# Gated linear attention before a SoLU block: the first loads split by halves of heads over two queues, narrower products of ones, and part of w_in requested later

## The chip, the cores and the metric

One NeuronCore of a Trainium2 chip (trn2). The metric is the device time of one execution in microseconds (us); lower is better. A NeuronCore has five engines with a queue of instructions each: TensorE (PE, matrix products), VectorE (DVE), ScalarE (ACT), GpSimd (POOL) and SyncE (SP), which in this kernel mostly issues DMAs. 16 DMA engines move the data. The engines run independently and wait for each other by semaphores.

## What is computed

Inputs q, k, v and alpha have the shape 4 x 8 x 768 x 48 (batch, head, position, width). The first block is a recurrence over the positions, the second works on the 3072 tokens of 8 x 48 = 384 numbers that come out of it.

```python
for t in range(S):
    state = alpha[:, :, t, :, None] * state + np.einsum('bhd,bhe->bhde', k[:, :, t], v[:, :, t])
    y[:, :, t] = np.einsum('bhd,bhde->bhe', q[:, :, t], state)
...
h = x @ w_in                                  # 3072 x 384 times 384 x 1024
e = np.exp(h - h_max)
solu = h * (e / (np.sum(e, axis=-1, keepdims=True) + 1e-09))
ln = (solu - mu) / np.sqrt(var + 1e-06) * g_ln
return (ln @ w_out).astype(np.float32)        # 1024 x 384
```

The weights w_in, w_out and g_ln reach the kernel in double or single precision; here w_in and w_out are double, and the kernel makes single precision of them itself.

## The kernel before

The positions are cut into six groups of 128 (g = 0 to 5). Group 0 has a prologue of its own, written out by hand in one fixed order; later groups' attention is interleaved with the second block of the group before, by a table of steps. The order of each engine's instructions is the order in which the program writes them; nothing reorders them afterwards. Where a buffer or a semaphore is shared, the instruction waits.

The prologue of group 0, which the change touches, goes as follows.

- Loads. `load_first` (L146) requests alpha, then k, then q for the first 128 positions on SP's queue, each in two requests of two batches. A request of two batches is 16 x 128 pieces of 192 bytes, one for each head and position. `load_v` (L176) requests v in four. ACT's queue brings ident, mask, parity and g_rows (L671 to L675), four small constants. Then `fetch` (L578) requests the first pieces of w_in: `fetch(0, 3)` into slot 3 of `room`, `fetch(1, 4)` into slot 4, `fetch(2, 1, 2)` two pieces into slots 1 and 2. Each is three requests.
- `warm` (L452) multiplies a tile of ones by itself 14 times on PE. A single-precision product passes twice, so these are 28 passes. The result is not used.
- `turned` (L164) turns a loaded tile [position, batch x head x width] so that the width lies on the partitions: 12 blocks of 4 batches, each a product with ident. Blocks 0 to 7 are the first 32 numbers of heads 0 to 7. Blocks 8 to 11 are the other 16 numbers of pairs of heads; they are first gathered by an ACT copy, `ends_of` (L155). The results are three PSUM tiles of four blocks each: tp_a0 (heads 0 to 3), tp_a1 (heads 4 to 7), tp_a2 (the ends). For k and q they are tp_k and tp_q.
- Alpha's three tiles are copied to aT by ACT (L703), and DVE runs a scan over each (`scan_back`, L204), which gives the products of alpha from the end of the group. `alpha_over` (L196) checks on ACT that alpha is at most 1. After `inverses` (a reciprocal, L213), `scan_on` scans a second time (L204 too), for each tile.
- DVE multiplies the turned k by the first scan (kT, L712) and the turned q by the second (qv and qe, L721). From qe, ACT makes two masked versions (`apart`, L245).
- `scores` (L278) multiplies kT and qv on PE, in two halves of heads; `masked` (L289) sets the upper part to zero on DVE, with a quarter of it on ACT and POOL (`masked_apart`, L297 and L298). `read_values` (L333) multiplies by v, and ACT copies the result to x (L363).
- `bits(0)` makes single precision of the first piece of w_in with five DVE instructions (L616 to L630); `keys_back` (L303) turns the keys back.
- Then the second block starts: `up_mm` (L394) multiplies w_in and x for eight slices f of 128 columns, the first two of which need the first piece of w_in only. `bits(1)` makes the second piece, and so on. `down` (L507) is the second product, with w_out.

The order in the prologue is then: loads, `warm(14)`, alpha turned, copied and scanned, k turned, `alpha_over`, `inverses`, a scan, kT, a scan, `warm(4)`, q turned, qv, qe, `apart`, a scan, qv, the scores, the masks, `bits(0)`, `read_values`, `keys_back`, `up_mm`.

Of the kernel before, what the change touches and what calls it, by code (L numbers as in the profile page):

```python
# [16 lines left out]
P = 128  # L17
# [15 lines left out]
def fast_path(ctx, tc, q, k, v, alpha, moe_w_in, moe_w_out, moe_g_ln, out):  # L33
# [12 lines left out]
    nc = tc.nc  # L46
    B, H, S, D = q.shape
# [4 lines left out]
    NP = H // 2  # L52
    NB = H + NP
# [8 lines left out]
    def pool(name, bufs, **kw):  # L62
        return ctx.enter_context(tc.tile_pool(name=name, bufs=bufs, **kw))
# [8 lines left out]
    ps_o = pool("ps_o", 2, space=PS)  # L72
# [4 lines left out]
    ident = const.tile([P, P], FP, name="ident")  # L77
    mask = const.tile([P, P], FP, name="mask")
    ones = const.tile([P, P], FP, name="ones")
    small_ones = const.tile([P, 32], FP, name="small_ones")  # L80
    parity = const.tile([P, 2], FP, name="parity")
# [9 lines left out]
    slots = [room[:, 1536 * i : 1536 * i + 1536] for i in range(6)]  # L91
# [7 lines left out]
    an = const.tile([P, H, TQ, D], FP, name="an")  # L99
# [39 lines left out]
    def by_token(x):  # L139

        return x.rearrange("p h u d -> p (h u d)").rearrange("p (b h d) -> p b h d", b=B, h=H)

    def load_first(src, dst, g):
        t = slice(g * P, (g + 1) * P)
        for b in range(0, B, 2):
            nc.sync.dma_start(  # L146
                out=by_token(dst)[:, b : b + 2].rearrange("p b h d -> p (b h) d"),
                in_=src[b : b + 2, :, t].rearrange("b h p d -> p (b h) d"),
            )

    def ends_of(src, tag=None):

        ends = ring.tile([P, T4], FP, name=tag) if isinstance(tag, str) else lots[tag][:, 0:T4]
        ends = ends.rearrange("p (b d) -> p b d", b=B)
        nc.scalar.copy(out=ends.rearrange("p b (h d) -> p b h d", h=H), in_=by_token(src)[:, :, :, E0:D])  # L155
        return ends

    def turned(src, ends, out, blocks=range(NB)):

        x = by_token(src)  # L160
        for j in blocks:
            for b in range(B):
                cols = x[:, b, j, 0:E0] if j < H else ends[:, b, E0 * (j - H) : E0 * (j - H) + E0]
                nc.tensor.matmul(  # L164
                    out[j // NP][32 * b : 32 * b + 32, j % NP], lhsT=cols, rhs=ident, start=True, stop=True,
                    tile_position=(0, 32 * b), skip_group_check=True,
                )
# [38 lines left out]
    def scan_back(g, i):  # L206

        part = slice(NP * i, NP * i + NP)
        scan(h4[:, part], aT[:, part], unit, True)
# [5 lines left out]
    def scan_on(g, i):  # L215
        part = slice(NP * i, NP * i + NP)
        scan(aT[:, part], aT[:, part], seed[:, part], False)
# [25 lines left out]
    def apart():  # L243
        for i in range(2):
            nc.scalar.mul(  # L245
                out=qv[:, H : 2 * H, 0:P].rearrange("p (j i) t -> p j i t", i=2)[:, :, i], in_=qe[:, :, 0:P],
                mul=parity[:, i : i + 1],
            )
# [16 lines left out]
    def quarter(b):  # L265
        return slice(32 * b, 32 * b + 32)

    def banks(name, shape, n=B):
        return [ps_a.tile([P] + shape, FP, tag=f"a{b}", name=f"{name}{b}") for b in range(n)]

    def scores(g, half, a=None):
        a = a or banks("a", [NP, P])
        for last in range(2):
            for i in (0, 2, 1, 3):
                h = half * NP + i
                kb, qb = (H + h // 2, H + h) if last else (h, h)
                for b in range(B):
                    nc.tensor.matmul(  # L278
                        a[b][:, i], lhsT=kT[quarter(b), kb], rhs=qv[quarter(b), qb, 0:P], start=not last and not i, stop=bool(last),
                        tile_position=(32 * b, 0), skip_group_check=True,  # L280
                    )
        masks[half] = a
# [163 lines left out]
                nc.scalar.copy(out=d["p"][:, i], in_=d["q"][i])  # L446
            d["unit"] = small_ones

    def warm(n, ps=ps_o, tag="o"):
        t = ps.tile([P, 512], FP, tag=tag, name="warm")  # L450
        for i in range(n):
            nc.tensor.matmul(t[:, 0:P], lhsT=ones, rhs=ones, start=True, stop=True)  # L452

    def token_sums(g):

# [111 lines left out]
    def fetch(i, slot, n=1):  # L567

        kind, f = pieces[i]
        w = n * F // (2 if kind else KC)  # L570
        raw = room[:, 1536 * slot : 1536 * (slot + n)].bitcast(U32).rearrange("p (c f w) -> p c f w", f=w, w=2)
        if kind:
            parts = [(slice(0, P), c, moe_w_out[(f + c) * P : (f + c + 1) * P, :]) for c in range(2)]
        else:
            parts = [(slice(0, P), c, moe_w_in[c * P : (c + 1) * P, f * P : f * P + w]) for c in range(KC)]
        for rows, c, src in parts:
            if float64:
                nc.sync.dma_start(out=raw[rows, c].rearrange("p f w -> p (f w)"), in_=src.bitcast(U32))  # L578
            else:
                dst = w_out[rows, f + c, 0:DM] if kind else w_in[rows, c, f * P : f * P + w]  # L580
                nc.sync.dma_start(out=dst, in_=src)
        for m in range(n):
            raws[i + m] = raw[:, :, w // n * m : w // n * (m + 1)]
# [81 lines left out]
    def inline(x, name):  # L665
        return nc.inline_tensor(np.ascontiguousarray(x, np.float32), name=name).ap()

    load_first(alpha, an, 0)
    nc.vector.memset(mone, -1.0)
    nc.scalar.activation(out=far[:, 0, 1:2], in_=mone, func=AF.Exp)  # L670
    nc.scalar.dma_start(out=ident, in_=inline(np.eye(P), "ident_c"))  # L671
    nc.scalar.dma_start(out=mask, in_=inline(np.triu(np.ones((P, P))), "mask_c"))
    odd = np.arange(P) // E1 % 2
    nc.scalar.dma_start(out=parity, in_=inline(np.stack([1 - odd, odd], 1), "parity_c"))
# [10 lines left out]
    nc.gpsimd.memset(kg, 0.0)  # L685
    load_v(0)
    fetch(0, 3)
    fetch(1, 4)
    fetch(2, 1, 2)
    nc.vector.memset(ones, 1.0)  # L690
    nc.vector.memset(small_ones, 1.0 / 32)
    nc.vector.memset(mhalf, -0.5)
# [2 lines left out]
    def three(name, where):  # L695
        return [pool.tile([P, NP, P], FP, tag=tag, name=f"{name}{i}") for i, (pool, tag) in enumerate(where)]


    warm(14)
    t = three("tp_a", [(ps_a, "a0"), (ps_a, "a1"), (ps_a, "a2")])  # L700
    turned(an, ends_of(an, 1), t)
    for i in range(3):
        nc.scalar.copy(out=aT[:, NP * i : NP * i + NP, 1:SW], in_=t[i])  # L703
        scan_back(0, i)
    t = three("tp_k", [(ps_a, "a3"), (ps_h, "h"), (ps_h, "h")])
# [7 lines left out]
    scan_on(0, 0)  # L713
    t = three("tp_q", [(ps_a, "a0"), (ps_o, "o"), (ps_o, "o")])
    warm(4, ps_a, "a1")
    turned(qn, ends_of(qn, 3), t, (*range(NP), *range(H, NB), *range(NP, H)))
    for i in (0, 2, 1):
        if i == 1:
            scan_on(0, i)
        part = slice(NP * i, NP * i + NP)  # L720
        nc.vector.tensor_tensor(  # L721
            out=qe[:, :, 0:P] if i == 2 else qv[:, part, 0:P], in0=t[i], in1=aT[:, part, 1:SW], op=ALU.mult
        )
        if i == 2:
            apart()
    scores(0, 0)
    t = [x.tile([P, NP, P], FP, tag=n, name="a_" + n) for x, n in ((ps_h, "h"), (ps_o, "o")) for _ in range(2)]
    scores(0, 1, t)
# [193 lines left out]
    for g in range(1, G + 1):  # L922
# [10 lines left out]
        for s in range(FC):  # L933
# [18 lines left out]
            if todo:  # L952
                n, half = todo.pop(0)
# [24 lines left out]
    def compare(out, x, bound, op):  # L978
# [6 lines left out]
        out=chunks[:, :, 2], in0=sums[:, :, 2], scalar=0.25, in1=sums[:, :, 3], op0=ALU.mult, op1=ALU.is_le  # L985
# [6 lines left out]
    else:  # L992
# [9 lines left out]
        out=bad, in0=all_ok[0:1, 0:1], scalar1=float(P * ends[-1]), scalar2=None, op0=ALU.is_lt  # L1002
# [415 lines left out]
def kernel(tc, *args):  # L1418

    with ExitStack() as ctx:  # L1420
        taken = fast_path(ctx, tc, *args)
    with tc.If(taken > 0):
        general_path(tc, *args)
# [30 lines left out]
```

## Time and profile before

| | |
|---|---|
| median of 3 runs | 368.23 us (368.16 to 368.46) |
| the profiled execution's own time | 367.97 us |
| its span (first to last instruction of the program) | 366.2 us |
| granted clock of TensorE, mean | 1.00 |
| PE busy, share of the span | 357.8 us, 98% |
| start of the first up-projection (L394) | 28.39 us |

The tables that follow come from this one profiled execution. In rows of the timeline, the first number is the start in us from the beginning of the span, the second the length in us, then come engine, line of the code, operation, the tile written and the tiles read, the shape and how many instructions are merged in the row; a bracket says how long the engine had been idle before and what ended the wait. PEld is the loading of weights into PE, which overlaps PE's own work. A name such as SPq is the queue of an engine that issues DMAs.

### The profile page before, as it was taken

The page shows a single profiled execution, that of the slowest core. Times are in us where ns is not written, and L with a number is a line of the kernel's source. Part 1 is how long each engine was busy: PE and PEld are TensorE (multiplying, and loading weights), DVE is VectorE, ACT ScalarE, POOL GpSimd, SP SyncE. Part 2 cuts the span into 40 slices and gives each one's busy share as a digit, 9 for nine tenths or more (in the row PEclk, how much of TensorE's full clock was granted, in tenths as well). Part 3 has the DMA queues.
Part 4 walks back from the last instruction along what each step waited for, and adds up shares of the span by engine and source line. Part 5 has one row for each costly group of instructions (what it writes and reads, how often), then busy time and mean ns, then how long its engine had stood idle before and what let it go on. Part 6 is the DMA issues. An engine that isn't in the chain of part 4 may idle for free. (4 is left out here: it accounts for less than half of the span.)

```text
span 366.2 us, 10036 instructions
## 1 busy us (share of the span) xinstructions
PE 357.8 (98%) x4341; PEld 215.0 (59%) x4341; DVE 245.0 (67%) x375; ACT 146.4 (40%) x260; POOL 132.2 (36%) x129
## 2 busy tenths in 40 slices
PE   8899999999999999999999999999999999999994
PEld 8784355666755566566575456475556565555552
DVE  0999989979998797936675935766946314345420
ACT  3647878182645262252521252431241132222110
POOL 7020000004449963774133764232773121233300
PEclk9999999999999999999999999999999999999999
DMA  9995995326196409463035354004041000000011
GB/s 180 183 338 152 204 309 124 88 67 159 50 234 141 109 21 180 85 152 94 21 92 112 83 121 126 3 25 88 21 107 55 0 25 0 24 21 22 23 47 51
DMA packets 72871, 36.06 MB, mean 98 GB/s; under 512 B 48232, under 2 KB 70000, under 8 KB 72816
## 3 DMA queue, kind: packets, MB, share of 16 engines
q1 hardware_dynamic: 71792, 34.39, 39.8%
q10 hardware_dynamic: 1024, 0.92, 0.8%
q8 instruction: 36, 0.59, 0.7%
q14 instruction: 19, 0.16, 0.2%
HBM read 25.30 MB, written 4.72 MB: 82 GB/s over the span
## 5 line engine op out<-in xcount | busy, mean ns | idle before, releaser
L507 PE MATMUL o<-w_out,room 128*128 128x385 f32 x384 | 134.0, 492 | 0.0
L394 PE MATMUL h<-x,w_in 128*128 128x512 f32 x288 | 131.7, 597 | 0.5 <-DVE g_col L642 0.5
L507 PEld LDWEIGHTS o<-w_out,room 128*128 128x128 f32 x384 | 71.0, 189 | 54.7 <-issue 13.1
L394 PEld LDWEIGHTS h<-x,w_in 128*128 128x128 f32 x288 | 53.2, 189 | 58.6 <-issue 48.5
L409 DVE TENSOR_TENSOR room<-h,e 128x512 f32<-128x512 f32 x40 | 27.5, 689 | 72.9 <-ACT e L408 72.9
L408 ACT ACTIVATE e<-h 128x512 f32<-128x512 f32 x40 | 24.0, 599 | 100.2 <-PE h L394 100.2
L427 POOL TENSOR_TENSOR p<-p,e 128x512 f32<-128x512 f32 x30 | 43.7, 1458 | 20.0 <-ACT e L408 19.9
L412 ACT ACTIVATE u<-room 128x512 f32<-128x512 f32 x40 | 25.2, 630 | 38.3 <-DVE room L409 38.3
L546 POOL TENSOR_TENSOR r<-sums,mhalf 128x1 f32<-128x1 f32 x20 | 14.8, 741 | 69.7 <-DVE sums L537 69.4
L289 DVE TENSOR_TENSOR sT<-a,mask 128x512 f32<-128x512 f32 x43 | 26.7, 681 | 8.0 <-PE a L278 7.9
L204 DVE TENSOR_TENSOR_SCAN hT<-aT,unit 128x516 f32<-128x516 f32 x18 | 24.4, 1399 | 7.6 <-ACT aT L703 7.5
L204 DVE TENSOR_TENSOR_SCAN aT<-aT,seed 128x516 f32<-128x516 f32 x18 | 27.4, 1551 | 0.2
L225 POOL TENSOR_TENSOR kT<-kT,hT 128x1024 f32<-128x1024 f32 (+1 forms) x8 | 14.2, 1800 | 32.7 <-DVE kT L179 32.7
L427 DVE TENSOR_TENSOR p<-p,u 128x512 f32<-128x512 f32 x30 | 22.5, 749 | 5.1 <-ACT u L412 5.1
L278 PEld LDWEIGHTS a<-qv,kT 32*128 32x128 f32 x704 | 21.4, 186 | 7.0 <-issue 2.6
L278 PE MATMUL a<-qv,kT 32*128 32x128 f32 x704 | 23.9, 278 | 0.4 <-POOL qv L253 0.3
L212 POOL COPY fend<-hT 128x12 f32<-128x12 f32 x6 | 3.1, 509 | 55.9 <-DVE hT L204 55.9
L333 PE MATMUL y<-sT,vn 128*32 128x128 f32 x768 | 22.6, 273 | 0.2 <-DVE sT L289 0.2
L333 PEld LDWEIGHTS y<-sT,vn 128*32 128x32 f32 x768 | 20.7, 110 | 1.6 <-issue 1.0
L196 ACT ACTIVATE sq<-an,mone 128x1536 uint8<-128x1536 f32 x12 | 18.9, 1572 | 0.2
L548 ACT ACTIVATE o_sb<-o,r 128x384 f32<-128x384 f32 x16 | 9.3, 582 | 18.5 <-POOL r L546 18.5
L261 POOL TENSOR_TENSOR state<-state,lot 128x384 f32<-128x384 f32 x10 | 8.8, 903 | 13.1 <-DMA lot<-qv 13.1
(148 smaller groups left out, 374.3 us busy)
## 6 DMA issues: line engine op xcount, KB each, us to landing
vn<-in_v_dram SPq DMA_DIRECT2D x24, 192.0 KB, 4.7
an<-in_alpha_dram SPq DMA_DIRECT2D x20, 192.0 KB, 4.1
out_dram<-o_sb SPq DMA_DIRECT2D x20, 192.0 KB, 1.9
room<-in_moe_w_out_dram SPq DMA_DIRECT2D x8, 384.0 KB, 5.5
kn<-in_k_dram SPq DMA_DIRECT2D x16, 192.0 KB, 5.6
qn<-in_q_dram SPq DMA_DIRECT2D x16, 192.0 KB, 4.1
lot<-qe SPq DMA_DIRECT2D x40, 64.5 KB, 2.1
lot<-qv SPq DMA_DIRECT2D x20, 129.0 KB, 2.4
```

What stands on the lines that cost most here:

```text
L196: nc.scalar.activation(out=sq, in_=x, func=AF.Relu, scale=sign, bias=mone, accum_out=over[:, g, i : i + 1])
L204: nc.vector.tensor_tensor_scan(out=o, data0=a, data1=s, initial=1.0, op0=ALU.mult, op1=ALU.add)
L278: nc.tensor.matmul(a[b][:, i], lhsT=kT[quarter(b), kb], rhs=qv[quarter(b), qb, 0:P], start=not last and not i, stop=bool(last), tile_posit ...
L289: nc.vector.tensor_tensor(out=sT[:, b, half * NP : half * NP + NP], in0=a[b], in1=mask[:, None, :].to_broadcast([P, NP, P]), op=ALU.mult,)
L333: nc.tensor.matmul(y_bank(b)[quarter(r), a], lhsT=lhsT, rhs=rhs, start=(b, r) not in begun, stop=stop, tile_position=(row, 32 * r), skip_g ...
L394: nc.tensor.matmul(h, lhsT=w_in[:, a, f * P : (f + 1) * P], rhs=d["x"][:, a].rearrange("p b t -> p (b t)"), start=(a == 0), stop=(a == KC ...
L408: nc.scalar.activation(out=e, in_=h, func=AF.Exp)
L409: nc.vector.tensor_tensor(out=u, in0=h, in1=e, op=ALU.mult)
L412: nc.scalar.activation(out=u2, in_=u, func=AF.Square)
L427: eng.tensor_tensor(out=p, in0=d[0][i] if f == 1 else p, in1=d[f][i], op=ALU.add)
L507: nc.tensor.matmul(d["o"][:, 0 : DM + 1], lhsT=u_of(g, f)[:, b * P : b * P + P], rhs=w_out[:, f], start=(f == 0), stop=(f == FC - 1), skip ...
L546: nc.gpsimd.tensor_tensor(out=r, in0=s[:, 3:4], in1=mhalf, op=ALU.pow)
```

## The change

Four edits, all in the prologue of group 0.

- The request for ident is the first on ACT's queue. After it, alpha is requested in eight parts instead of two: first heads 0 to 3 of each batch, then heads 4 to 7; batches 0 and 1 on SP's queue, batches 2 and 3 on ACT's. The table load of ACT and the requests for mask, parity and g_rows come behind.
- `warm` has a width; the first 14 products are of 92 instead of 128 columns. The later `warm(4)` stays at 128.
- Blocks 0 to 3 of alpha are turned, copied and scanned before the gathering copy of the ends. The other eight blocks are turned after it.
- `fetch(1, 4)` and `fetch(2, 1, 2)` move behind `apart`. A copy of one column of parity into slot 4 stands before them, so that the first of these requests has to wait for ACT to reach it. The other loads keep their order.

```diff
-    def warm(n, ps=ps_o, tag="o"):
+    def warm(n, ps=ps_o, tag="o", w=P):
         t = ps.tile([P, 512], FP, tag=tag, name="warm")
         for i in range(n):
-            nc.tensor.matmul(t[:, 0:P], lhsT=ones, rhs=ones, start=True, stop=True)
+            nc.tensor.matmul(t[0:w, 0:w], lhsT=ones[:, 0:w], rhs=ones[:, 0:w], start=True, stop=True)
...
-    load_first(alpha, an, 0)
+    nc.scalar.dma_start(out=ident, in_=inline(np.eye(P), "ident_c"))
+    for h in (slice(0, NP), slice(NP, H)):
+        for b in range(B):
+            queue = nc.sync if b < 2 else nc.scalar
+            queue.dma_start(out=by_token(an)[:, b, h], in_=alpha[b, h, 0:P].rearrange("h p d -> p h d"))
     nc.vector.memset(mone, -1.0)
     nc.scalar.activation(out=far[:, 0, 1:2], in_=mone, func=AF.Exp)
-    nc.scalar.dma_start(out=ident, in_=inline(np.eye(P), "ident_c"))
     nc.scalar.dma_start(out=mask, in_=inline(np.triu(np.ones((P, P))), "mask_c"))
...
     fetch(0, 3)
-    fetch(1, 4)
-    fetch(2, 1, 2)
...
-    warm(14)
+    warm(14, w=92)
     t = three("tp_a", [(ps_a, "a0"), (ps_a, "a1"), (ps_a, "a2")])
-    turned(an, ends_of(an, 1), t)
     for i in range(3):
+        if i == 0:
+            turned(an, None, t, range(NP))
+        elif i == 1:
+            turned(an, ends_of(an, 1), t, range(NP, NB))
         nc.scalar.copy(out=aT[:, NP * i : NP * i + NP, 1:SW], in_=t[i])
         scan_back(0, i)
...
         if i == 2:
             apart()
+            nc.scalar.copy(out=slots[4][:, 0:1], in_=parity[:, 0:1])
+            fetch(1, 4)
+            fetch(2, 1, 2)
```

## Prediction

> **What bounds the kernel now.** I read the page first, then a table by stage (the windows view), then the timeline of the first 30 us, last the DMA packets of that stretch.
>
> ```profile
> PE 357.8 (98%) x4341; PEld 215.0 (59%) x4341; DVE 245.0 (67%) x375; ACT 146.4 (40%) x260; POOL 132.2 (36%) x129
> ```
>
> TensorE is busy 98% of the span. The windows view says where the rest lies (columns: window, length, then busy us and instructions of PE, PEld, DVE, ACT, POOL, then clock, DMA share and GB/s):
>
> ```profile
> 0.00:6.80 6.80, 5.45 (x32) 5.06 (x32) 0.29 (x5) 1.49 (x2) 6.21 (x12) 1.00 0.89 167
> 6.80:12.10 5.30, 4.38 (x153) 4.12 (x157) 3.46 (x3) 3.90 (x6) 0.49 (x1) 1.00 1.13 186
> 28.40:366.00 337.60, 332.53 (x3748) 192.26 (x3748) 225.69 (x345) 132.40 (x238) 122.69 (x113) 1.00 0.37 88
> ```
>
> From 28.4 us on, where the up-projection starts, PE works 332.5 of 337.6 us, so that part is bound by PE and is only shifted by what happens before it. Only the first 28.4 us are open, and every 0.1 us by which the first up-projection (L394) starts sooner is 0.1 us of the total. In the prologue the chain goes by these rows of the timeline (start, length):
>
> ```profile
> 6.83 1.83 PE L164 MATMUL tp_a<-ident,an 128*32 128x128 f32 x58 [0.30 <-DMA an<-in_alpha_dram]
> 8.64 3.48 DVE L204 TENSOR_TENSOR_SCAN hT<-aT,unit 128x516 f32<-128x516 f32 x3 [7.54 <-ACT aT L703]
> ...
> 14.99 0.96 PE L164 MATMUL tp_q<-ident,qn 128*32 128x128 f32 x26 [0.20 <-DMA qn<-in_q_dram]
> 15.41 1.22 DVE L204 TENSOR_TENSOR_SCAN aT<-aT,seed 128x516 f32<-128x516 f32 x1
> 16.74 0.69 DVE L721 TENSOR_TENSOR qv<-tp_q,aT 128x512 f32<-128x512 f32 x1
> 17.35 0.68 DVE L721 TENSOR_TENSOR qe<-tp_q,aT 128x512 f32<-128x512 f32 x1
> 17.73 2.45 PE L278 MATMUL a<-qv,kT 32*128 32x128 f32 x64
> 18.07 1.34 ACT L245 ACTIVATE qv<-qe,parity 128x512 f32<-128x512 f32 x2 [2.42 <-DVE qe L721]
> ...
> 23.91 0.76 DVE L616 TENSOR_SCALAR lot<-room 128x768 uint32<-128x768 uint32 x1
> 28.39 2.81 PE L394 MATMUL h<-x,w_in 128*128 128x512 f32 x6 [0.46 <-DVE g_col L642]
> ```
>
> VectorE sits idle 7.54 us until alpha is turned, then runs almost without a gap to 28.2: three scans to 12.12, one more, keys, a scan to 16.64, qv, qe, and so on. The last step before L394 is the making of w_in's first piece (L616 to L630, 23.91 to 28.24). So **two clocks run side by side**: the VectorE chain, which alpha starts, and the load queue, which brings q at 14.95 and the first piece of w_in at 23.52 (last of its three transfers, by the landings in the trace). Slack of the second against the first is small: q's third block was turned at 16.93 and used at 17.35; w_in was there 0.39 us before its use.
>
> ```profile
> GB/s 0 0 0 18 178 271 265 274 236 233 225 210 221 222 219 199 226 226 208 227 218 227 97 21 124 255 260 246 199 202 223 104 157 214 127 183 198 133 117 131
> ```
>
> This row is the DMA rate in half-microseconds from 0 to 20 us: the engines work from 1.85 us without rest except for a hole near 11.5. The loads are a stream at its own pace.
>
> [...] SP spends 1.67 to 1.76 us on each 2048-packet request between 4.7 and 8.2, but only 1.47 on one after the hole, so it can issue faster than it does. [...] between 2.75 and 3.0 us alpha's packets fall from 270 to 183 per quarter while 77 of ident's pass. [...] Here products of ones start at 1.08 and the clock rises at 4.71, 3.63 us later; it never falls.
>
> **The change, part by part.**
> Narrower products (L452). 28 passes of 128 columns come every 213 ns until 4.71, then every 112. With 92 columns I scale to 92/128: 153 and 80 ns. 23 passes are through by 4.71, the other five by 5.15. PE is free at about 5.2 instead of 6.19. The 36 columns fewer cost nothing: no result is used.
>
> Alpha by halves on two queues. Alpha is 4096 packets of 192 B either way: two requests on SP become four on SP and four on ACT. The first half with ident is 2048 + 128 packets; before, the first 2048 and ident had landed at 4.64. I take 4.7. So PE turns heads 0 to 3 from 5.2: 32 passes at 27.3 ns (the spacing in tp_a) and 0.27 to drain end at 6.35; the copy (L703, 0.59) ends at 7.0, and the first scan starts at 7.05 instead of 8.64. The other half lands with all of alpha; mask, parity and g_rows (136 packets of 512 B, 128 tiny) now queue behind it, which by their 21 to 26 ns each over 16 engines is worth 0.25: 6.55 instead of 6.79. ACT copies the ends after aT0 (7.0 to 7.6), tp_a1 ends at 7.7 and is copied to 8.35, tp_a2 ends at 8.8 and is copied to 9.45. Scans at 7.05, 8.4, 9.55, ending at 10.75: **1.37 us sooner than 12.12**. Reciprocal, scan, three key products and scan keep their 4.5 us and end at 15.3 (before 16.64).
>
> ACT's queue. It now issues ident, four of alpha, then loads its table (1.28), then mask, parity, g_rows at 0.45 to 0.69 each. The built order shows reused semaphores: the fourth alpha request waits for ident (landed 3.72 before), mask, parity and g_rows for the second to fifth alpha requests. I put the last at 5.1 + 0.7 = 5.8, ahead of the copy at 6.4: cost nothing, covered by PE; if alpha's fifth request lands 0.6 later, the copy is late by as much, which the next paragraph swallows. On SP the first request for k waits for the first of alpha (about 3.6, instead of issuing at 2.6); some 2000 alpha packets are still queued then, so the engines don't run dry.
>
> What is late next. If q stays at 14.95, its first block is turned at 16.06 (qv 0.64 sooner), its third at 16.93: qe starts at 17.0, **0.35 sooner**. ACT's two products, the second halves of the scores (which in the trace start at 18.84 and 19.46, each 0.05 after one of these), masks and L616 all move by that 0.35: L616 at 23.56, with its data at 23.52. So of 1.37 us only 0.35 comes through unless the stream itself moves; past that, each 0.1 us of q and w_in is 0.1 us. Both ends for the stream: no move (the packets and the engines are the same), and 1.2 sooner (if SP's queue had been the limit: its 2048 fewer packets at 1165/us are 1.76 us, less about 0.6 for the waits). I take 0.25, the worth of mask and its fellows out of alpha's way plus the ident request 0.16 earlier, less what they cost k again.
>
> Later half of w_in's first requests. Six requests on SP wait for a one-column ACT copy (bounded by 0.2, the smallest ACT row) after L245, at about 19.2 instead of 17.94. They queue behind the first piece, which lands till 23.5, and were landed at 24.2 to 29.5; 2 us after issue is 21.3, so they still follow the stream. First use at 28.2 and 32.95. Cost nothing; cover is 2.7 us. Behind them SP has only a request of 29.7. ACT is idle from 19.4 to 20.3, so its copy delays nobody.
>
> Sum: 0.35 + 0.25 = **0.6 us**. The profiled execution took 367.97 with a span of 366.2 (1.8 around it), so 367.4 by that; the median of the runs is 368.23, so 367.6.
>
> **Rivals.** (A) The stream was held by SP's queue, and two queues free it: q and w_in land 0.6 to 1.2 sooner, the gain is 0.95 up to the 1.37 of the scans, time 367.1. For it: after the hole packets run at 340 per quarter-microsecond, from 5 to 9 us at 287. Against: the slow packets take 18 to 19 ns, the fast ones 15, so it is the engines that are slower. (B) The loads come no sooner or a little later (two queues in turn, other instruction fetches: one of 16 KB at 9.52 held one DMA engine for 1.26 us[...]): gain 0 to 0.3, 368.1. (C) Slower: PE's clock falls. After tp_a PE will wait from 8.8 to k's 10.5, 1.7 us instead of 0.9. [...] Then turning k takes 5.2 instead of 2.6 us, against some 0.8 of slack: 1.8 lost less 0.6 gained, 369.4. [...] That the change doesn't do what it says I exclude: the built order has the requests and copies where the diff puts them.
>
> **How the numbers follow.** Forecast (stream 0 to 0.4 sooner, 367.5 to 367.9; likeliest 367.6): 0.50. A: 0.31. B: 0.11. C and mishaps like it: 0.08. A measurement of this kernel can tell about 0.2%, 0.74 us, from no change. Faster by more than that (under 367.49): A and a quarter of the forecast, 0.43. Within: the rest of the forecast and B, 0.48. Slower: C and a little of B, 0.09. The range leaves out C and the last of A: 366.8 to 368.5.
>
> **What would show it.** Right: the first scan near 7.05 and the third ending near 10.8; qe near 16.8, waiting for PE's tp_q and no more for VectorE; L616 near 23.3; L394 near 27.8; from there on the same 337.6 us to the end. Wrong: q landing before 14.2 (A), a first scan later than 7.7 (ACT's queue held by g_rows), products at 213 ns past 5.2 or turns at 55 ns (clock), L616 waiting for a DMA, or the last 337.6 us changing length.

## Result and profile after

| | before | after |
|---|---|---|
| median of the runs made side by side | 368.15 us (367.66 to 369.10, 22 runs) | 369.02 us (367.67 to 370.45, 22 runs) |
| ratio, 95% interval | | 1.0022 [1.0014, 1.0030] |
| the profiled execution's own time, span | 367.97 us, 366.2 us | 369.18 us, 367.4 us |
| start of the first up-projection (L394) | 28.39 us | 27.96 us |

The kernel became 0.22% slower. The forecast was 367.6 us with a range up to 368.5; the measured 369.02 lies above it. Note the spread: the fastest run after, 367.67, is as short as the fastest before, 367.66, but the runs after lie over 2.8 us and those before over 1.4. A second measurement of the same changed kernel is among the experiments; it gave less. Medians and ratios leave out runs in the chip's slower state, two runs of a single kernel below.

TensorE's line of the page, after. Its busy time fell by 0.6 us while the span grew by 1.2, so PE does nothing more than before; it waits.

```profile
PE 357.2 (97%) x4341; PEld 214.5 (58%) x4341; DVE 245.7 (67%) x375; ACT 146.2 (40%) x261; POOL 132.1 (36%) x129
```

The table by stage, after (columns as before; the last stage begins with the first up-projection):

```profile
0.00:6.80 6.80, 5.72 (x66) 5.46 (x66) 0.29 (x5) 1.60 (x3) 6.21 (x12) 1.00 0.86 165
6.80:12.10 5.30, 3.38 (x113) 3.00 (x114) 4.34 (x5) 3.40 (x6) 0.68 (x2) 1.00 1.20 199
27.97:367.20 339.23, 332.92 (x3748) 192.28 (x3748) 226.20 (x345) 132.18 (x238) 122.58 (x113) 1.00 0.37 88
```

By 6.8 us PE has done 66 passes, as was meant, where before had 32. But the last stage, from the up-projection on, has the same 3748 passes and takes 339.2 us and not 337.6. The prologue of after, in rows of the timeline:

```profile
5.54 1.37 PE L164 MATMUL tp_a<-ident,an 128*32 128x128 f32 x38
6.69 0.58 ACT L707 COPY aT<-tp_a 128x512 f32<-128x512 f32 x1 [1.77 <-PE tp_a L164]
7.38 1.23 DVE L204 TENSOR_TENSOR_SCAN hT<-aT,unit 128x516 f32<-128x516 f32 x1 [6.28 <-POOL kg L688]
8.86 2.36 DVE L204 TENSOR_TENSOR_SCAN hT<-aT,unit 128x516 f32<-128x516 f32 x2 [0.25 <-ACT aT L707]
...
16.03 0.69 DVE L725 TENSOR_TENSOR qv<-tp_q,aT 128x512 f32<-128x512 f32 x1 [0.29 <-PE tp_q L164]
16.90 0.69 DVE L725 TENSOR_TENSOR qe<-tp_q,aT 128x512 f32<-128x512 f32 x1 [0.18 <-PE tp_q L164]
17.62 1.34 ACT L245 ACTIVATE qv<-qe,parity 128x512 f32<-128x512 f32 x2 [2.06 <-DVE qe L725]
...
23.47 0.76 DVE L616 TENSOR_SCALAR lot<-room 128x768 uint32<-128x768 uint32 x1
```

The first scan starts at 7.38 (before 8.64), the scans end at 11.22 (12.12), and qv and qe now wait for PE's turning of q, so VectorE is ahead of the loads. Apart (L245) stands at 17.62 (18.07), the first piece of w_in at 23.47 (23.91): all 0.45 us sooner. That holds up to the up-projection. PE's rows from there on, after:

```profile
28.47 2.31 PE L394 MATMUL h<-x,w_in 128*128 128x512 f32 x5
30.71 1.57 PE L371 MATMUL kv<-vn,kg 128*32 128x48 f32 x128
32.20 2.41 PE L394 MATMUL h<-x,w_in 128*128 128x512 f32 x5
35.95 8.42 PE L394 MATMUL h<-x,w_in 128*128 128x512 f32 x19 [1.33 <-issue]
44.30 1.92 PE L439 MATMUL quarters<-sT,ones 128*32 128x512 f32 x16
```

Before, the second slice and all that follow are one unbroken row of 24 passes:

```profile
32.63 10.57 PE L394 MATMUL h<-x,w_in 128*128 128x512 f32 x24
43.12 1.92 PE L439 MATMUL quarters<-sT,ones 128*32 128x512 f32 x16
```

Now PE stops after five passes of the second slice, one before its end, for 1.33 us. "issue" as the releaser means that no instruction, semaphore or load is seen on which PE waited: weights and x are there, and the next pass is the sixth of a sum of six into a tile that it already holds. Everything after it is late by 1.18 us at 44.30 against 43.12. The list of PE's waits puts it second of all, and before's list has no such entry:

```profile
PE tp_k L164 <- DMA kn<-in_k_dram: 1.7, 1, 1.7
PE h L394 <- issue: 1.3, 1, 1.3
```

What lies in that moment is in the DMA view. On queue 8 it has a kind "instruction", with 36 packets of 16 KB in the whole span, in every trace of this study; in before they start from 9.52 to 359.44 us. PE has 4341 passes, 121 to a packet, and the places where it waits without a visible cause lie 254 passes apart, with one more such packet between the two (at 27.46 in before), so some 127 to a packet. From this estimate I take these packets to be PE's. Cut into stretches, after's DMA traffic is, from 29.7 to 33.5 us and then from 33.5 to 34.5 us:

```profile
q1 hardware_dynamic: 1056, 0.95, 87.3%
...
q1 hardware_dynamic: 1230, 0.23, 115.2%
q8 instruction: 1, 0.02, 5.8%
```

One packet of instructions starts at 33.51, takes 0.93, and PE goes on 1.51 us after its end, at 35.95. Before, the packet in the same place started at 32.44 and took 0.92; 1.51 after that is 34.87, and PE passed the place at 34.88 without stopping. If the delay is the same, before had nothing to spare. So my theory for the experiments was: **PE waits for a block of its own instructions**, which is transferred while it runs and comes late behind the data of w_in and w_out.

### The profile page after: what moved, and what is told of

Its sections match the earlier page's. It is cut to its first block, busy times and chain, and to the rows that moved or that the text cites. A ratio compares the mean times of both kernels' runs of the same rounds, so it can differ in the third digit from the quotient of the medians.

```text
span 367.4 us, 10047 instructions
## 1 busy us (share of the span) xinstructions
PE 357.2 (97%) x4341; PEld 214.5 (58%) x4341; DVE 245.7 (67%) x375; ACT 146.2 (40%) x261; POOL 132.1 (36%) x129
## 5 line engine op out<-in xcount | busy, mean ns | idle before, releaser
L394 PE MATMUL h<-x,w_in 128*128 128x512 f32 x288 | 131.9, 597 | 1.8 <-issue 1.3
L394 PEld LDWEIGHTS h<-x,w_in 128*128 128x128 f32 x288 | 53.1, 189 | 60.3 <-issue 50.5
L333 PE MATMUL y<-sT,vn 128*32 128x128 f32 x768 | 22.6, 273 | 0.2 <-DVE sT L289 0.2
L333 PEld LDWEIGHTS y<-sT,vn 128*32 128x32 f32 x768 | 20.8, 110 | 1.6 <-issue 1.0
```

Source lines behind the costliest of these rows:

```text
L333: nc.tensor.matmul(y_bank(b)[quarter(r), a], lhsT=lhsT, rhs=rhs, start=(b, r) not in begun, stop=stop, tile_position=(row, 32 * r), skip_g ...
L394: nc.tensor.matmul(h, lhsT=w_in[:, a, f * P : (f + 1) * P], rhs=d["x"][:, a].rearrange("p b t -> p (b t)"), start=(a == 0), stop=(a == KC ...
```

## Experiments

I number PE's passes from the start of the program (the first up-projection begins behind pass 593 in both kernels). Two places will matter: pass 478, within the product of the masks with v (y, L333), and pass 732, the last of the second slice (L394). "Transfer A" and "transfer B" are the last packets of instructions ahead of these. Ratios are to before, run side by side.

**Later w_in requests: taken out, and alone.** First, after with

```
+    fetch(1, 4)
+    fetch(2, 1, 2)
     nc.vector.memset(ones, 1.0)
...
-            nc.scalar.copy(out=slots[4][:, 0:1], in_=parity[:, 0:1])
-            fetch(1, 4)
-            fetch(2, 1, 2)
```

> The changed kernel with the second and third request groups for w_in back in their old place, right behind the first. Theory (late requests): the 1.33 us in which TensorE waits for nothing that the profile shows, before the last pass of the second slice (L394), is a wait for its own instructions, and the block of instructions comes late because the moved w_in requests stand before it on its DMA engine. Then the wait is gone, the fifth transfer of the instruction queue starts near 32.3 instead of 33.5, and the time is 0.4 to 0.6 us under the kernel before. Rival (early products): TensorE only reaches the end of its block 0.43 us sooner while the block comes when it always came; then the wait stays at 1 us or more, and the time is 0.5 to 1 us over the kernel before.

Measured 368.20 us, ratio 1.0002 [0.9993, 1.0011]. The loss is gone, but no gain has come in its place. Its timeline shows why:

```profile
22.47 0.64 PE L333 MATMUL y<-sT,vn 128*32 128x128 f32 x14 [0.20 <-DVE sT L289]
24.51 3.04 PE L333 MATMUL y<-sT,vn 128*32 128x128 f32 x102 [1.40 <-issue]
```

The wait at pass 732 is gone, another of 1.40 us of the same kind stands at pass 478, behind transfer A (22.08). Second, before with these late requests and nothing else of the change:

> The kernel before with the later w_in requests alone. Theory (late requests): the wait before the last pass of the second slice appears, 0.6 to 1.3 us, and the time is as much over the kernel before. Rival (early products): no such wait, time within 0.2 us of the kernel before, since TensorE keeps its old pace.

Measured 369.62 us, 1.0038 [1.0018, 1.0057]: slower by themselves, with waits at both places in its trace (0.46 and 0.90).

**Does the wait belong to a count of instructions?** Two fewer or two more products of ones at the start move every later instruction by four passes in the count, without touching a load.

```
-    warm(14, w=92)
+    warm(12, w=107)      # the other: warm(16, w=80)
```

> The changed kernel with 12 products of 107 columns instead of 14 of 92: the same 1290 columns and the same time, but 8 TensorE instructions fewer ahead of everything else. If TensorE waits for a block of instructions, the end of the old block now falls 4 passes later in the program, 1.7 us later in time at 0.43 a pass; the wait of 1.33 shrinks to nothing, or moves to the fourth pass of the third slice and is under 0.3; time 0.4 to 0.6 us under the kernel before. If the wait belongs to that product (its data, a buffer), it stays before the last pass of the second slice at 1.3, and the time stays 0.9 over.

> The changed kernel with 16 products of 80 columns: the same 1280 columns, but 8 TensorE instructions more. If TensorE waits for a block of instructions, the wait moves 4 passes up, to the first or second pass of the second slice, and grows by up to 1.7 to about 3 us; time 2 to 2.8 us over the kernel before. If the wait belongs to the product, nothing moves, 0.9 over.

Measured 368.48 us, 1.0009 [0.9998, 1.0020], and 371.08 us, 1.0079 [1.0050, 1.0108]. The directions hold, the sizes don't: fewer passes gave no gain, more cost far more than four passes can explain. The place, though, is exact. With two products fewer and with two more, the wait in y stands here:

```profile
22.34 0.85 PE L333 MATMUL y<-sT,vn 128*32 128x128 f32 x18 [0.20 <-DVE sT L289]
24.17 2.08 PE L333 MATMUL y<-sT,vn 128*32 128x128 f32 x65 [0.97 <-issue]
```

```profile
22.34 0.62 PE L333 MATMUL y<-sT,vn 128*32 128x128 f32 x10 [0.20 <-DVE sT L289]
24.08 2.18 PE L333 MATMUL y<-sT,vn 128*32 128x128 f32 x72 [1.12 <-issue]
```

Behind 14 passes in the variant above, behind 18 with four passes fewer ahead, behind 10 with four more: always at pass 478 of the program, whatever product that is. A wait for one product's data would have moved with that product. The second place keeps its count too: with two products fewer PE runs through pass 732, with two more it waits 0.54 us there, now behind one pass of the second slice and not five. In that trace a third wait of the kind, 0.91 us, stands at pass 2260, 1782 passes behind 478, fourteen times some 127. The three make 2.57 us, and the profiled execution is 2.23 longer than before's; where the longer runs of this kernel lose more is not shown.

**Moving the places far.** The 28 passes of the products of ones as 8 wide ones move everything by 20 passes:

```
-    warm(14, w=92)
+    warm_wide(4, 80)      # matmul(t[0:80, 0:320], lhsT=ones[:, 0:80], rhs=ones repeated 4 times)
```

> After, with its 14 products of ones, 92 columns each (28 passes), written as 4 products of 80 rows by 320 columns (8 passes of about the same total length). Every later TensorE instruction thereby stands 20 passes earlier in the count of instructions, and the ends of instruction blocks fall 20 passes later in the program. Theory (a block of TensorE's instructions is transferred on demand and comes late behind the data of w_in and w_out): the end of a block at pass 732 moves from the second slice of up_mm into the fifth, some 8.6 us later in the work, where its transfer has had time to land: no wait there; the wait at pass 478, if any, falls 0.5 us later in the program and is smaller by that or gone. Time 367.4 to 367.8 (0.1 to 0.4% under before), with a narrower spread than after's. Rival (the late w_in requests themselves cost the time, through data that come late or a slower DMA): the time stays 0.9 over before, near 369.0, and the loss of about 1.3 us is found in another wait.

> Before, with its 14 products of ones of 128 columns (28 passes) written as 4 products of 112 rows by 448 columns (8 passes of the same total length); nothing else differs. Theory (instruction blocks): before stands at zero slack at pass 732 (its block arrived as it was needed), so moving the ends of blocks 20 passes later takes away the waits that some of its executions have: 367.7 to 368.0, 0.0 to 0.12% under before. Rival (the position of blocks does not matter): level with before within 0.03%, and the same spread.

> The two edits together: after with the 4 wide products of ones and with w_in's requests in their old place. Theory (instruction blocks): neither of the two block ends meets a late block; the 0.43 us that the prologue gains reaches the end: 367.3 to 367.7, level with the variant that has the wide products alone within 0.1%. Rival (late requests cost time by themselves): this one is about 0.9 us faster than the variant with wide products alone.

Measured: 368.44 us, 1.0011 [0.9999, 1.0024]; 369.39 us, 1.0033 [1.0021, 1.0045]; 369.30 us, 1.0033 [1.0021, 1.0045]. As a forecast of time the theory failed three times. The first shows the mechanism at its best: no wait over 0.13 at either place, the first up-projection at 27.85, and PE ahead of before by 0.57 us as far as 123 us; then 0.87 is lost at once, 0.56 of it in a wait for POOL, in a stage that the change doesn't touch. In the other two the wait in y grew:

```profile
21.68 2.03 PE L333 MATMUL y<-sT,vn 128*32 128x128 f32 x46
25.43 2.59 PE L333 MATMUL y<-sT,vn 128*32 128x128 f32 x82 [1.72 <-issue]
```

That is the third of them: behind 46 passes of y, 20 more than the 12 + 14 of the variant without wide products, pass 478 again. My mistake was to think that moving the end of a block gives its transfer more time. The transfer moves too; only its place in the traffic changes, and here it fell on a worse one (transfer A at 23.11, where after with early w_in has 22.08).

**Taking the traffic away.** Four kernels leave out w_out's first requests, which lie ahead of transfer B, or hold them back, and with them the requests for the second group's k, q and alpha behind them:

```
-            fetch(4, 3)
+            raws[4] = slots[4].bitcast(U32).rearrange("p (c f w) -> p c f w", c=2, w=2)
```

> After, leaving out the load of the first piece of w_out (the down projection takes w_in's bits in its place, so part of the weights is not the reference's; the amount of work on every engine is the same). Theory (the data of w_out, asked for between 27 and 33 us, keep the fifth transfer of TensorE's instructions back): that transfer starts at or before 31.5 us instead of 33.51, and the wait of 1.33 us before pass 732 is gone or under 0.3; time about 0.7 to 1.2 us under after. Rival (the transfer is late by itself, whatever data is on the way): it starts near 33.5 again and the wait is about 1.3.

```
+            nc.scalar.copy(out=slots[3][:, 0:1], in_=parity[:, 0:1])
             next_state(0)
             fetch(4, 3)
```

> After, with one ScalarE copy of one column into the buffer of the first piece of w_out, put ahead of its requests, so that these and the requests for the second group's k, q and alpha behind them on SP's queue leave at about 33.5 us and not at 29.3. Nothing is left out. Theory (the data of w_out hold back the block of TensorE's instructions that begins at pass 732): its transfer starts by 31.6 us and the wait at pass 732 is gone, as in the run without that piece of w_out; what is left is the wait at pass 478, 0 to 1.4 us by chance. Time 0.3 to 1.0 under after measured beside it, 368.0 to 368.7 where after has 369.0. Rival (the loss sits mainly at pass 478, and 732 was the accident of one profiled execution): level with after within 0.1%.

> The same copy in the variant of after that has w_in's requests in their old place (it measured level with before). Theory: only the wait at pass 478 is left, so at most 0.2% faster than that variant was: 367.7 to 368.2, level with before or up to 0.1% under it. Rival (w_out's requests 4 us later cost time of their own, through k, q and alpha of the second group): 0.1% or more over before.

> Before, with the same copy ahead of w_out's first requests. Theory: before's block at pass 732 arrived just as it was needed, and waits there in some executions only, so there is little to gain: 367.7 to 368.1, 0 to 0.1% under before. Rival (w_out's requests 4 us later cost time of their own): 0.1% or more over before.

Transfer B now started at 31.55 and 31.31 us in the two made from after (33.51), at 31.50 in the one with w_in early (31.22, so no sooner) and at 31.71 in the one made from before (32.44). None of the four waits at pass 732. The DMA view of the second one from 31.3 to 32.3 us has the instructions alone:

```profile
q8 instruction: 1, 0.02, 5.8%
```

and its PE rows run through, 0.37 us ahead of before at pass 732:

```profile
22.50 3.58 PE L333 MATMUL y<-sT,vn 128*32 128x128 f32 x116 [0.20 <-DVE sT L289]
...
28.02 2.81 PE L394 MATMUL h<-x,w_in 128*128 128x512 f32 x6 [0.32 <-ACT kg L305]
30.76 1.57 PE L371 MATMUL kv<-vn,kg 128*32 128x48 f32 x128
32.26 4.99 PE L394 MATMUL h<-x,w_in 128*128 128x512 f32 x11
```

So at that place the theory holds for after. The times don't help: 370.25 us, 1.0071 [1.0055, 1.0088] without the piece; 374.45 us, 1.0180 [1.0163, 1.0197], 374.23 us, 1.0172 [1.0156, 1.0188] and 374.52 us, 1.0176 [1.0152, 1.0200] with the copy. The expected times were missed by some 2 us without the piece and 6 us with the copy. With the copy, k, q and alpha of the second group, which stand behind w_out on SP's queue, came late too, which may be part of it; and all four have one more wait, of 2.05 to 2.72 us, which before and after lack. In the second one it is:

```profile
75.45 1.08 PE L164 MATMUL tp_q<-ident,u 128*32 128x128 f32 x32 [2.71 <-DVE kT L799]
```

Its cause I didn't settle; it came with every edit that takes w_out's requests from their place in the order. From these runs, and the next three, only what lies before 44 us is used, but for one observation on the clock at the end.

**The same requests in another order**, k of the second group ahead of w_out:

```
-            fetch(4, 3)
             load_first(k, kn, 1)
+            fetch(4, 3)
```

> After, with the first two requests of w_out moved behind the second group's two of k on SP's queue; the same requests, nothing added. w_out's leave at about 32.6 us and not at 29.3, k's 0.9 sooner, q's and alpha's as before. Theory (w_out's data hold back the block that begins at pass 732): its transfer starts by 31.8 us and there is no wait at pass 732; w_out's bits are first worked on at about 44 us, so its 3 us cost nothing. The 0.4 us of the prologue come through in the executions without a wait at pass 478: median 367.6 to 368.1, 0.3 to 1.2 under after as it was first measured and 0 to 0.15% under before. Rival (any data that moves at that time holds it back, k's as well as w_out's): the transfer starts near 33 again, with a wait of 0.8 to 1.3 there, and the time is after's, 368.2 to 369.0.

> Before, with the same exchange of w_out's and k's requests. Theory: before waits at pass 732 in some executions only, so at most 0.1% is to be had: 367.7 to 368.1. Rival (the exchange itself costs or brings time by way of the data): more than 0.1% off before on either side.

> After with w_in's requests in their old place and the same exchange. Theory: it waits at pass 478 if anywhere; 367.7 to 368.2, and the variant with w_in late, which in its executions with an early third transfer (20.3 to 20.6 us) has no wait there, is as fast or up to 0.15% faster. Rival (w_in's late requests cost time by themselves): this one is 0.1% or more faster than that with w_in late.

Measured 371.12 us, 1.0077 [1.0053, 1.0101]; 371.53 us, 1.0098 [1.0085, 1.0111]; 370.23 us, 1.0053 [1.0036, 1.0071], each with 2.03 to 2.05 us of the wait at the same tp_q. The rival was right on the point in question: transfer B started at 33.06 in the first, with 0.41 of wait, and at 32.33 and 32.30 in the others, so with k's data in the place of w_out's it comes no sooner than in before.

**After once more.**

> After once more, word for word, for a second profiled execution and as the neighbour of the variant with w_out's requests later. Theory (TensorE waits for blocks of its instructions, whose arrival differs from execution to execution): the waits of over 0.3 us that the profile gives no other cause for stand at passes 478 and 732 again, one or both, and the time is 368.7 to 369.3. Rival (something else makes after slow): this execution is as slow, but without a wait at those two passes.

Measured 368.25 us (367.92 to 372.58, 13 runs) beside 368.10, ratio 1.0008 [0.9989, 1.0028]. The wait is there again, at the same pass, but shorter:

```profile
32.18 2.41 PE L394 MATMUL h<-x,w_in 128*128 128x512 f32 x5
35.38 1.98 PE L394 MATMUL h<-x,w_in 128*128 128x512 f32 x4 [0.79 <-issue]
```

The time expected, 368.7 to 369.3, was too high. The first measurement excludes level with before, this one includes it; on both, after is not faster.

**Each part alone.** After with only half of the late requests, before with only the narrower products, before with only alpha by halves:

```
+    fetch(1, 4)
...
-            nc.scalar.copy(out=slots[4][:, 0:1], in_=parity[:, 0:1])
-            fetch(1, 4)
+            nc.scalar.copy(out=slots[1][:, 0:1], in_=parity[:, 0:1])
             fetch(2, 1, 2)
```

> After, with the three requests of the second piece of w_in in their old place and only the three larger ones of the third and fourth pieces held until ScalarE has written into their buffer. Theory (waits for blocks of TensorE's instructions decide): the prologue's 0.4 us as in after, a wait at pass 478 or 732 by chance, in the sum 0 to 1.3: 367.9 to 368.7. If the lateness of w_in itself costs (rival), this lies halfway between after and the variant with w_in early, 0.05 to 0.1% over before.

```
-    warm(14)
+    warm(14, w=92)       # before
```

> Before, with the 14 first products of ones 92 columns wide and not 128; nothing else. By the prediction's steps: TensorE is free about 0.5 us sooner, but alpha's first half is not there sooner, so that alone brings little: first product of up_mm 0.0 to 0.15 us sooner. Theory: 368.0 to 368.3, level with before. Rival (a shorter run of products at the start delays the rise of the clock and the work after it): 0.1% or more over before, seen as a later rise of the clock.

```
-    warm(14, w=92)
+    warm(14)             # after with w_in's requests in their old place
```

> Before, with identity and first alpha by halves requested first on two queues and the transposes by halves; products of 128 columns and w_in's requests as in before. Theory: the prologue gains 0.2 to 0.45 us by pass 351 with or without the narrower products, and a wait at pass 478 may take it back in the same execution: 367.8 to 368.3. Rival (the narrower products carry the prologue's gain): nothing is gained by pass 351 and the time is level with before or over it.

Measured 368.38 us, 1.0004 [0.9994, 1.0014]; 368.15 us, 1.0004 [0.9994, 1.0014]; 368.38 us, 1.0001 [0.9990, 1.0011]: all level with before. Alpha's part alone brings the whole gain of the prologue: its last scores are 0.45 us ahead of before at 20 us, the narrower products alone bring none (the first up-projection at 28.38). One profiled execution each stands behind this, and in alpha's the clock rose early, at 4.16 us. In before the products of 128 columns come every 213 ns ahead of the rise and every 112 behind it, so with a later rise they would keep PE longer; that is an estimate, which no run here shows. And alpha's gain ends in y:

```profile
22.40 0.65 PE L333 MATMUL y<-sT,vn 128*32 128x128 f32 x14 [0.20 <-DVE sT L289]
23.23 3.04 PE L333 MATMUL y<-sT,vn 128*32 128x128 f32 x102 [0.19 <-issue]
```

PE is there early, waits, and goes on at 23.23; before passes the same instruction at 23.25.

All profiled executions that have their places in the same passes of work, from the traces (start of the transfer in us, then PE's wait in us):

| kernel | A | wait at 478 | B | wait at 732 |
|---|---|---|---|---|
| before | 20.99 | none | 32.44 | none |
| before, narrower products | 21.36 | 0.21 | 33.00 | 0.36 |
| before, late w_in | 21.90 | 0.46 | 33.06 | 0.90 |
| before, w_out late | 21.60 | 0.51 | 31.71 | none |
| before, k first | 21.45 | 0.27 | 32.33 | none |
| alpha alone | 20.91 | 0.19 | 30.68 | none |
| after, early w_in | 22.08 | 1.40 | 31.22 | none |
| after, half of w_in early | 22.10 | 1.34 | 31.62 | none |
| after, early w_in, k first | 21.08 | 0.39 | 32.30 | 0.35 |
| after, early w_in, w_out late | 21.69 | 0.62 | 31.50 | none |
| after | 20.37 | none | 33.51 | 1.33 |
| after again | 20.33 | none | 33.02 | 0.79 |
| after, k first | 21.87 | 0.66 | 33.06 | 0.41 |
| after, w_out late | 20.58 | none | 31.31 | none |
| after, without w_out's piece | 21.59 | 1.00 | 31.55 | none |

Down to pass 478, the last five are nearly the same program, and transfer A starts anywhere from 20.33 to 21.87. Two executions of the very same kernel, after, have B at 33.51 and 33.02. So the arrival differs from execution to execution.

Wherever PE waited over 0.25 us at pass 478, it went on 2.2 to 2.5 us after A's start. The four executions without a wait pass it as closely behind A: 1.31 us after its end in before, 1.43 to 1.48 in the three of after, where waits end 1.27 to 1.60 after a transfer. So no kernel here has slack at pass 478, before included, and what the prologue gains passes this place only in executions in which A starts sooner as well.

## Why the prediction was wrong

**The step that failed** is the first one: "From 28.4 us on ... that part is bound by PE and is only shifted by what happens before it", and with it "every 0.1 us by which the first up-projection (L394) starts sooner is 0.1 us of the total". The up-projection started 0.43 us sooner, and the stage behind it took 1.6 us longer (339.2 for 337.6). PE stopped with its data at hand. By the theory it waited for instructions, which come by DMA as well, at their own time (36 packets on queue 8; transfer B at 32.44 in before and 33.51 in after). Before had no slack at passes 478 and 732: at the second, arrival at 34.88 was just enough. After needed the block 0.43 sooner, and its transfer started 1.07 later. Rival B had one such packet, at 9.52, as something that holds data back. That data hold the instructions back I didn't consider.

**The cost put at nothing**, "Later half of w_in's first requests ... Cost nothing; cover is 2.7 us", failed too. I counted who uses w_in, and none of them was late. But before with this part alone is 0.38% slower, and after without it is level with before, as is after with only the larger three of the six requests late. The exact path from those requests to transfer B isn't settled: w_in's last data landed at 30.74 (before 29.54) and w_out's requests, gone at 29.26, were on the way; leaving out w_out's first piece brought B forward to 31.55, and with k's data in its place B was late again. But alpha alone has both w_out and k at their usual time and B at 30.68, and the narrower products alone, with w_in's requests in their old place, have B at 33.00 and a wait of 0.36. So data ahead of the transfer delayed it often here, not always, and that late w_in costs time is shown by the times, not by one path in the traces.

**The scans.** Predicted: first at 7.05, end at 10.75. Measured 7.38 and 11.22. The mis-sized terms: the clock rose at 5.40 and not at 4.71, behind the last product of ones, so PE turned alpha from 5.54 (5.2). That rise differs between executions (4.98 in the second of after), which the prediction took as fixed; and alpha's last request landed at 7.10, 0.31 later than before and not 0.24 sooner (6.55); why is not shown. A gain of 0.90 for 1.37.

**What is late next.** Right in kind and size: qv 0.71 and qe 0.45 sooner (0.64 and 0.35 predicted), both now waiting for q. Narrower products, told as what frees PE at 5.2, weren't needed in the executions profiled: alone they bring nothing, and without them alpha's part has the same 0.45.

**The stream.** I took 0.25 sooner; q landed at 14.87 (14.95) and k at 10.78 (10.50). These didn't move, within 0.3; only the third request of w_in's first piece came sooner, at 22.90 (23.52), and that is no gain to count, as before with nothing but narrower products had it at 22.16. Rival A, SP's queue as the limit, is refuted: 8 alpha requests on two queues brought alpha's last request no sooner (7.10 for 6.79) and q by 0.08 only. One reading offered for it was wrong, too: the request of 1.47 us "after the hole" is one of v's, of 1024 packets and not 2048, so it doesn't show that SP can issue faster.

**Rivals B and C.** B (no gain) is what the versions without late w_in requests show, by another cause than I gave: the gain is made, and then waits for transfer A. C (the clock) did not happen: PE waited 1.7 us for k, and the clock stayed at 1.00. But it was not far off. In before with k first, PE was busy 1.38 of the 3.41 us from 69.32 on, and the 3.41 us behind them ran at half clock:

```profile
69.32:72.73 3.41, 1.38 (x20) 0.63 (x22) 3.27 (x6) 0.71 (x2) 0.46 (x3) 1.00 0.51 105
72.73:76.14 3.41, 3.41 (x32) 2.11 (x21) 3.05 (x4) 0.00 (x0) 0.00 (x0) 0.50 0.00 0
```

The same came after 0.83 us of work in after with early w_in and w_out late. After has 1.72 in the 3.41 us around its wait for k (8.81 to 12.22), and no other 3.41 us around the wait have less; so C was missed by 0.34 us of work or less, an estimate from 1.72 and 1.38.

**The sum.** Predicted were 0.35 by the chain and 0.25 by the stream, and then a stage of unchanged length. In the profiled execution: 0.45 by the chain and nothing by the stream, so 0.43 sooner at the up-projection; the step to pass 732 takes 1.93 us where a step takes 0.43, so 1.07 later there; 1.18 at 44 us, and 1.2 in the span (367.4 for 366.2). In the second one of after: 0.45 sooner, 0.79 of wait, 0.50 later at pass 732, 0.6 in the span (366.8). No version tried beats before; the fastest medians are level with it.

## What to carry to other kernels

Where an engine is busy 98% of the time, look at what could still stop it: cut the DMA view at the instruction packets and note how long before its use each one arrives. Here that slack was nothing in before (34.87 against 34.88 at pass 732): 0.43 us moved forward gave no gain at the end (369.02 for 368.15), and w_in's requests moved alone cost 0.38%, with waits of 0.46 and 0.90 in the trace. An "issue" wait that stays at one count of instructions when a few are added or taken away ahead of it (pass 478 here, with four passes fewer and four more) points to such a block, and as it differs between executions (1.33 and 0.79 us in the two of after), one profile doesn't give its size.

## What the runs showed of the hardware that I hadn't expected

- What I take for PE's instructions comes in 36 transfers of 16 KB on queue 8; each takes 0.88 to 1.69 us in before and after, and where PE waited, it went on 1.3 to 1.6 us after the end (1.51 in after at pass 732). The two places of waiting lie 254 passes apart.
- The same instructions on the same data differ by up to 1 us between executions, with transfer A at 20.33 to 21.87: five of the executions are of kernels alike up to pass 478, and three of them have no wait there, two have 0.66 and 1.00.
- The first products start at 1.08 us in all 20 traces, and the clock rises anywhere from 4.06 to 7.21 (4.71 in before, 5.40 and 4.98 in the two of after).
- Products of 320 or 448 columns in place of 92 and 128, at the same total, made nothing faster. Before with them was 0.33% slower [0.21, 0.45] in six runs. Its first transpose stood at 7.30 and not 6.12, but the clock rose only at 7.21 in that execution, so the wide products aren't shown to be the reason.
